# Sparse attention and a residual MLP on one core: w_tok in two halves, an identity made on GpSimd, and the order of the opening and of the weave

## The chip, the core and the metric

One core of a Trainium2 chip. Its engines run side by side, each through its own queue in order: PE (TensorE: matmuls and transposes, with weight loads shown as PEld), DVE (VectorE), ACT (ScalarE), POOL (GpSimd) and SP (SyncE, which only issues DMAs here). ACT and POOL also issue DMAs from their queues. The metric is the device time in microseconds (us) of one execution.

## The reference, cut to what matters

```
scores = q @ k.T / 8            # 4 batches, 8 heads, 768 tokens, 64 dims
scores = where(mask, scores, -1e9)   # per 32x32 block: window of 1, first and last
                                     # block, and 3 sampled blocks in each row of blocks
x   = softmax(scores) @ v            # heads side by side: (4, 768, 512)
a1  = alpha1 * x + beta1
u   = x + lam * einsum('ts,bsd->btd', w_tok, a1)
a2  = alpha2 * u + beta2
out = u + lam * (relu(a2 @ w_ch1) @ w_ch2)
```

w_tok is 768 x 768; w_ch1 is 512 x 2048 and w_ch2 is 2048 x 512. All inputs are float32 in DRAM; the work is done in bfloat16 and float16 with float32 sums.

## The kernel before, in words

Tokens are held as 128 partitions x 6. The 32 heads are worked in 16 pairs, numbered from 0; four pairs make a batch. The whole program is one list of instructions, written out in an order that lists in the file decide.

**Pairs 0 to 4** make the first stage. Each pair has 9 units, so there are 45 steps (the loop over `s`, L1089). A step issues the scores of one unit on PE (`emit_qk`, L583: k is the weight, 88 rows deep, since 24 rows of mask levels and block indicators lie under the 64 of q and k), the exp of the unit on ACT (`emit_exp`, L601, 128 x 1024), and two steps later the product with v (PV, L630), with a column of ones in `vext` that gives the row sums. Two PSUM buffers (`sp`) hold the scores, so the scores of step s wait for the exp of step s - 2. A finished head is scaled on DVE (`emit_finish`, L670 and L671) and then made into `a1pp` (L687, L688), on DVE or POOL as `A1V` says.

Between these, `PLAN` places every other job of the stage: a name and a time in steps. A job runs in the step of its whole part, ahead of PV where the fraction is under 0.5 and behind it otherwise. Among these jobs are the loads (`emit_load`, by POOL), the transposes of q and k through PSUM (`emit_tps`, L493, evicted by DVE at L499), the casts of v (`emit_lay`, L313), the mask rows of the other buffers (`emit_mask_rows`, L439), the mask as columns for later (`emit_mask_cols`, L508, L511; spread by POOL at L519), the broadcast of lam, alpha1 and beta1 over partitions (`emit_parts`, `emit_bcast`, L719 to L730), the transposes of w_tok (`emit_wtok_t`, L778, L779), the token mix of pairs 0 to 3 (`job_tok`, L795 to L810), the transposes of u (`job_ut` at L846, or a DMA transpose with `emit_uscale` at L870), and the loads and scaling of w_ch1 and w_ch2 (`emit_w1_load` L753, `emit_w2_load` L759, `emit_w2_use` L765). `OPEN` and `POUR` say how many f1 jobs follow each of the last three steps.

**Pairs 5 to 15** make the second stage. Their scores are 64 rows deep, from DMA transposes (`emit_tdma`), and a mask of zeros and ones is multiplied in on DVE (`emit_keep`, L618). The strings of `WEAVE` set the order, a string to three units: q the scores, x an exp, k a mask product, p PV of one block of keys (L653), f one f1 job (4 matmuls of 384 columns, L884, relu on ACT at L891), g one f2 job (4 matmuls of 512, L903, added to x by DVE at L912), T two chunks of the token mix (L819), d and v DMA transpose and scaling of u, L, Q, K and Y loads and layouts of later pairs, 0, 1 and 2 the jobs that PLAN has in that slot.

**The opening** (before and around step 0) loads head 0 of q, k and v by SP and ACT, the sampled blocks by SP, and by ACT one constant of 128 x 640 bytes that holds the identity for transposes and the fixed part of the mask (L346). Nine filler matmuls run on PE meanwhile (`emit_warm(9)`, L463). q is cast on DVE, k on ACT; six transposes (`emit_tps0`, L481) follow, with DVE's copies (L471). DVE finds the mask of blocks (L394, L402), and six copies on ACT and three on DVE turn it into mask levels and spread them over the rows under k (`emit_mask_part`, L420 and L412). POOL makes the ones of `vext` (L363) and the indicator rows under q (L368, L370).

Tiles in PSUM come from pools: `sp` with two buffers, `mm` with three, `op` with one. In the first stage every second head sums into an `mm` buffer.

Of the kernel before, what the change touches and what calls it, by code (L numbers as in the profile page):

```python
# [20 lines left out]
S = 768  # L21
# [16 lines left out]
OPEN = 42  # L38
UTD = [1, 1]
TDM = [1, 0]  # L40
A1V = [1, 0, 0, 1, 0, 0, 0, 1]
POUR = [3, 1, 1]
W1 = [
    "q f Y x f 0 f p k 1 f k f p x 2 f f k f f",
    "q L f x Q f f f k p x f p 0 k 1 p k 2",
    "q x g x f k k f 0 g 1 g k 2 K",
    "q Y Q k p K g p x x 0 f 1 s k 2 p k L f",
    "q 0 f x x g 1 g g k p k k 2",
    "q k s g p f x 0 f k 1 T x f p 2 k",
    "q 0 1 f p x k 2 p K T x L k p k",  # L50
    "q f x f 0 x T 1 p 2 Y k p k k Q",
    "q x f 0 k k g p x 1 s 2 g k d g",
]
W2 = [
    "q 0 p p p f d L x K f k v g 1 Q v g k x g g k 2",
    "q x 0 k f x g s 1 k 2 T T p p k T",
    "q d Y k p x g 0 1 2 g d g k x v p k",
    "q k L g x k 0 p g g 1 x p k 2 Q v",
    "q g x p g 0 x f f f Y k 1 f k 2 k f",
    "q 0 f k p x k f p f f f x 1 p p K f k f 2",  # L60
    "q f f x f f k 0 1 Q Y x p k g g 2 k s",
    "q 0 g g s k x f f 1 f 2 x k L f k p p",
    "q T f T T k 0 1 x x k K f f 2 f k p f f",
    "q p p p d s k x L d 0 x K k g k Y 1 f f 2 g",
    "q 0 x k Q g x 1 g p k 2 k p",
    "q k x v 0 1 p g k x k f g f g 2",
]
W3 = [
    "p p p f g v f s g T T T g g d g g g g d g g v g v g g f f f f f f",
    "f f f f f f f f f f f f g f f g f g f g f f g g f g f f g f f g g g f g",  # L70
    "f f g g g g g g g g g g g g",
]
WEAVE = W1 + W2 * (B - 2) + W3
ENG = {
# [16 lines left out]
    "tq1": 0,  # L91
}
PLAN = {
    "layv00": 0.29,
    "wtkl": 0.42,
    "warm1": 0.49,
    "loadv2": 0.58,
    "layk01": 1.22,
    "layq01": 1.25,
    "mask_cols": 1.5,  # L100
    "rows1": 2.08,
    "tps0": 2.52,
    "parts": 2.83,
    "mask1": 2.94,
    "w1_0": 2.96,
    "tq1": 4.55,
    "layv01": 4.3,
    "rows2": 4.5,
    "tk1": 4.82,
    "lv1": 5.01,  # L110
    "bcast0": 5.1,
    "rows3": 5.84,
    "loadk3": 6.08,
    "bcast2": 6.12,
    "loadv3": 7.02,
    "mask3": 7.41,
    "loadk2": 8.21,
    "loadq2": 8.52,
    "bcast1": 8.8,
    "loadq3": 9.23,  # L120
    "a1pp0": 9.37,
    "w1_2": 9.64,
    "w1_1": 10.3,
    "columns": 11.32,
    "wt2": 11.35,
    "wt1": 11.76,
    "wt5": 12.19,
    "lv2": 12.84,
    "wt4": 13.01,
    "wt0": 13.43,  # L130
    "loadv4": 13.94,
    "w1_3": 14.3,
    "tq2": 14.44,
    "loadq4": 14.54,
    "wt3": 15.31,
    "columns_use": 16.32,
    "tk2": 16.6,
    "tok0_0": 17.05,
    "tok0_1": 17.4,
    "tk3": 18.13,  # L140
    "loadk4": 18.23,
    "tok0_2": 20.0,
    "tq3": 20.4,
    "mask8": 20.72,
    "loadk5": 20.73,
    "mask2": 20.89,
    "tok0_3": 21.32,
    "tok0_4": 22.02,
    "lv3": 22.91,
    "mask6": 22.94,  # L150
    "mask0": 23.62,
    "tok0_5": 23.87,
    "loadq5": 24.3,
    "tok1_0": 24.53,
    "mask4": 24.64,
    "w2_0": 24.82,
    "mask7": 25.08,
    "lv4": 25.4,
    "tok1_1": 25.6,
    "tok1_2": 27.2,  # L160
    "loadv5": 27.53,
    "tok1_3": 27.74,
    "tok1_4": 28.91,
    "tok1_5": 29.7,
    "w2_2": 29.98,
    "mask5": 30.09,
    "tq4": 30.41,
    "mask15": 30.72,
    "udma0": 30.82,
    "tk4": 31.72,  # L170
    "udma1": 31.9,
    "w2_1": 32.02,
    "tq5": 32.51,
    "mask9": 32.65,
    "tok2_0": 33.91,
    "tk5": 34.64,
    "usc0": 34.69,
    "tok2_1": 34.88,
    "mask14": 34.9,
    "mask13": 35.48,  # L180
    "tok2_2": 35.71,
    "mask11": 35.79,
    "tok2_3": 36.37,
    "lam16": 37.24,
    "mask17": 37.68,
    "w2_3": 37.7,
    "mask16": 37.75,
    "tok2_4": 37.77,
    "mask10": 37.9,
    "tok3a_0": 38.34,  # L190
    "tok3a_1": 38.43,
    "tok2_5": 38.51,
    "tok3a_2": 38.52,
    "tok3a_3": 38.85,
    "tok3a_4": 39.48,
    "tok3b_0": 39.51,
    "tok3b_1": 39.52,
    "tok3b_2": 39.53,
    "tok3b_3": 39.54,
    "ut2": 39.85,  # L200
    "tok3a_5": 40.02,
    "mask12": 40.23,
    "tok3b_4": 40.23,
    "usc1": 40.28,
    "lv5": 40.42,
    "ut3_0": 40.8,
    "tok3b_5": 41.21,
    "cast3": 42.22,
    "lam2": 42.25,
    "lam3": 43.09,  # L210
    "ut3_1": 43.63,
    "lam1": 44.85,
    "lam10": 44.92,
    "lam9": 45.25,
    "lam7": 45.27,
    "lam0": 45.32,
    "lam11": 45.58,
    "lam6": 45.9,
    "lam13": 46.09,
    "lam5": 47.61,  # L220
    "lam14": 47.82,
    "lam4": 47.9,
    "lam8": 49.72,
    "lam12": 49.8,
    "lam15": 50.13,
}


# [1 line left out]
def kernel(  # L230
# [31 lines left out]
    kbi_np = np.tile(np.arange(NBLK, dtype=np.float32), (NBLK, 1))  # L262
    ms_np = np.concatenate([mstat_np] + [kbi_np] * NR, axis=1)

    const_np = np.zeros((P, P + 2 * (1 + NR) * NBLK), dtype=ml_dtypes.bfloat16)
    const_np[:, 0:P] = np.eye(P, dtype=ml_dtypes.bfloat16)
    const_np[0:NBLK, P:] = ms_np.view(ml_dtypes.bfloat16)
    const_dr = nc.inline_tensor(const_np, name="const_c")
    indq_dr = nc.inline_tensor(np.tile(indq_np, (1, 2)), name="indq_c")
    ident8_dr = nc.inline_tensor(np.eye(8, dtype=np.float32), name="ident8_c")  # L270

# [6 lines left out]
    def ptile(shape, dt, name):  # L278
        return pp.tile(shape, dt, name=name, tag=name)
# [4 lines left out]
    def copy_of(name):  # L284
        return (nc.vector.tensor_copy, nc.scalar.copy, nc.gpsimd.tensor_copy)[ENG[name]]
# [34 lines left out]
            :, 2 * n * NT * D : 2 * (n + 1) * NT * D  # L320
        ].rearrange("p (w x) -> p w x", w=2)
    sampi = ptile([P, 2 * NR], I32, "sampi")
    const = ptile([P, P + 2 * (1 + NR) * NBLK], BF, "const")
    identb = const[:, 0:P]
    ms = const[:, P:].bitcast(FP)
    NQB = 4
    qTs = [ptile([P, 2, S], BF, f"qTs{i}") for i in range(NQB // 2)]
    kTs = [ptile([P, 2, S], BF, f"kTs{i}") for i in range(NQB // 2)]
# [14 lines left out]
    load_first("q", q, 0, nc.sync)  # L343
    load_first("k", k, 0, nc.scalar)
    nc.sync.dma_start(sampi[0:NBLK, :], sampled_blocks.bitcast(I32))
    nc.scalar.dma_start(const[:], const_dr.ap())  # L346
    load_first("v", v, 0, nc.sync)
    load_first("k", k, 1, nc.scalar)
    load_first("q", q, 1, nc.sync)
# [9 lines left out]
        qTs[1][D : D + NBLK], indq_dr.ap().rearrange("r (w s) -> r w s", w=2)  # L359
    )  # L360
    warm = nc.const_aps.tensor(1.0, (P, DM), BF)
    for t in vexts:
        nc.gpsimd.memset(t[:, :, :, D : D + 1], 1.0)  # L363

    def emit_indicator():
        rows = qTs[0][D : D + NBLK]
# [37 lines left out]
        ms[0:NBLK, :].rearrange("q (r b) -> q b r", r=1 + NR),  # L404
        axis=mybir.AxisListType.X,
    )
    big = ptile([P, 1], FP, "big")
    nc.vector.memset(big[:], -BIG8)

    def level_rows(eng):  # L410
        if eng == 0:
            return lambda out, in_: nc.vector.tensor_scalar(  # L412
                out=out,
                in0=in_,
                scalar1=1.0,
                scalar2=BIG8,
                op0=ALU.subtract,
                op1=ALU.mult,
            )
        return lambda out, in_: nc.scalar.activation(  # L420
            out, in_, AF.Identity, bias=big[0:NBLK, :], scale=BIG8
        )

    def emit_mask_part(jp, copy):
        sl = kText[0][D : D + NBLK, ts(jp, 2 * P)]
        dst = sl.rearrange("q (o g r) -> q o g r", o=2, r=16)
        src = mbm[0:NBLK, :].rearrange("q (g m) -> q g m", m=3)
        m_of = (6 * np.arange(16) + 2 * jp) // BLK
        assert (m_of == (6 * np.arange(16) + 2 * jp + 1) // BLK).all()
        for m in range(3):  # L430
            lo, hi = np.searchsorted(m_of, [m, m + 1])
            shape = [NBLK, 2, NBLK // 3, int(hi - lo)]
            copy(
                out=dst[:, :, :, int(lo) : int(hi)],
                in_=src[:, :, m].unsqueeze(1).unsqueeze(3).broadcast_to(shape),
            )
# [14 lines left out]
    def mm_tile(shape=(P, DM), dt=FP):  # L451
        return psum.tile(list(shape), dt, name="mm", tag="mm", bufs=3)
# [316 lines left out]
    def emit_wtk_load():  # L769
        t = ap_.tile([P, NH, QC], BF, name="hts", tag="hts", bufs=2)  # L770
        wtks[0] = t[:, 0:12, :].rearrange("p (o w) n -> p o (w n)", o=NT)
        nc.gpsimd.dma_start(wtks[0], moe_w_tok.rearrange("(p o) s -> p o s", o=NT))

    def emit_wtok_t(os_):
        wtk = wtks[0]
        tps = mm_tile((P, NT, P), BF)
        for ot in range(NT):
            nc.tensor.transpose(tps[:, ot, :], wtk[:, ot, os_:S:NT], identb[:])  # L778
        nc.vector.tensor_copy(out=wtokT[:, os_, :], in_=tps[:])  # L779

    toks = {}
    ubfs = {}
# [203 lines left out]
            start_mlp(i // NP)  # L988

    emit_load(1)  # L990
    for m in (32, 64):
        nc.gpsimd.tensor_tensor(
            out=pick[0:96],
            in0=identb[0:96, 0:12] if m == 32 else pick[0:96],
            in1=identb[0:96, m : m + 12],
            op=ALU.add,
        )
    nc.gpsimd.memset(parts[:], 0.0)
    emit_mask_part(0, level_rows(ENG["mp0"]))
    emit_mask_part(1, level_rows(ENG["mp1"]))  # L1000
    emit_tps0(0)
    emit_warm(2)
    emit_mask_part(2, level_rows(ENG["mp2"]))

# [191 lines left out]
```

## Time and profile before

| | us |
|---|---|
| median of 3 runs (302.95 to 303.28) | 303.16 |
| the profiled execution | 303.09 |
| its span, first to last instruction | 301.4 |
| granted TensorE clock, mean | 0.998 |
| PE busy in the span | 295.3 |
| first exp on ACT starts | 7.36 |
| first scores of pair 5 on PE | 58.61 |
| last matmul of the program (L923) ends, about | 298.4 |

How to read it: "idle before" in a row is the time for which the engine did nothing ahead of the group, with what released it. A row of the timeline holds instructions of one kind in a row, so its second number is the length of the group, not of one. PE's busy time holds the fillers of the opening too, and the ends of matmuls are modelled; the distance of the starts of two matmuls tells more than their durations. Times between steps are therefore given from start to start.

### The profile page before, as it was taken

How to read it: one execution, taken by the hardware profiler on the slowest of the kernel's cores; microseconds unless marked ns; L12 is line 12 of the kernel's file. 1: busy time of each engine (PE TensorE's matmuls, PEld its weight loads, DVE VectorE, ACT ScalarE, POOL GpSimd, SP SyncE). 2: the span in 40 equal slices, each digit the busy share in tenths (PEclk: the TensorE clock that was granted, in tenths of full speed). 3: DMA queues.
4: the chain of work that ended last, by engine and by line, in shares of the span. 5: the costliest groups of instructions: out<-in, count | busy, mean ns of one | idle time of the engine just before them, and what ended most of it. 6: DMA issues, size and time to landing. Idle time of an engine off the chain costs nothing.

```text
span 301.4 us, 7199 instructions
## 1 busy us (share of the span) xinstructions
PE 295.3 (98%) x2976; PEld 184.5 (61%) x2996; DVE 193.1 (64%) x372; ACT 215.3 (71%) x314; POOL 113.1 (38%) x150
## 2 busy tenths in 40 slices
PE   8999999999999999999999999999999999999996
PEld 3687888655567556565665556565675664555543
DVE  3998799887758899845377779854476872000012
ACT  4999997999879775889778774889868610663310
POOL 8989589344328422613408501703206300000000
PEclk9999999999999999999999999999999999999999
DMA  6999999918297697970746693880411004100011
GB/s 191 188 198 204 204 165 186 155 29 129 68 132 115 111 140 120 130 159 2 115 78 111 115 171 89 124 165 3 63 32 23 37 35 122 37 0 35 37 70 70
DMA packets 57892, 31.34 MB, mean 104 GB/s; under 512 B 37952, under 2 KB 54764, under 8 KB 57732
## 3 DMA queue, kind: packets, MB, share of 16 engines
q0 software_dynamic: 16608, 14.22, 32.1%
q1 hardware_dynamic: 40820, 16.19, 25.5%
q10 hardware_dynamic: 432, 0.48, 0.5%
q8 instruction: 23, 0.38, 0.5%
q14 instruction: 9, 0.07, 0.1%
HBM read 29.83 MB, written 6.29 MB: 120 GB/s over the span
## 4 chain that ended last, share of the span: by engine, by line
PE 94%; ACT 3%; DMA 1%; issue 1%; DVE 0%; ACTq 0%
PE mm L884 28%; PE mm L903 26%; PE sp L583 10%; PE op L653 8%; PE mm L819 8%; PE mm L583 4%; PE mm L795 3%; ACT eT L601 2%; PE op L630 2%; DMA const<-const_c 1%; PE mm L923 1%; PE mm L630 1%; PE mm L493 1%; PE mm L778 1%; ACT kTs L420 1%
## 5 line engine op out<-in xcount | busy, mean ns | idle before, releaser
L601 ACT ACTIVATE eT<-sp,expb 128x1024 f16<-128x1024 f32 x111 | 118.4, 1118 | 3.0 <-PE sp L583 2.5
L891 ACT ACTIVATE hts<-mm 128x384 bf16<-128x384 f32 x128 | 62.1, 496 | 47.9 <-PE mm L884 47.1
L884 PE MATMUL mm<-uT,w1b 128*128 128x384 bf16 x512 | 92.6, 326 | 0.0
L618 DVE TENSOR_TENSOR eT<-eT,mask 128x1024 f16<-128x1024 f16 x99 | 74.8, 779 | 26.2 <-ACT eT L601 26.0
L903 PE MATMUL mm<-w2b,hts 128*128 128x512 bf16 x348 | 85.7, 379 | 1.1
L687 POOL TENSOR_TENSOR a1pp<-x_sb,vbc 128x384 bf16<-128x384 f32 x27 | 32.7, 1211 | 123.1 <-DVE x_sb L671 118.8
L884 PEld LDWEIGHTS <-w1b 128*128 128x128 bf16 x512 | 48.1, 98 | 35.0 <-issue 3.4
L903 PEld LDWEIGHTS <-hts 128*128 128x128 bf16 x368 | 34.0, 98 | 38.7 <-issue 4.0
L601 ACT ACTIVATE eT<-mm,expb 128x512 f16<-128x512 f32 x66 | 41.8, 686 | 18.5 <-PE mm L583 18.2
L912 DVE TENSOR_TENSOR ot<-x_sb,mm 128x512 f32<-128x512 f32 x23 | 15.7, 684 | 45.4 <-PE mm L903 45.4
L653 PEld LDWEIGHTS <-eT 128*128 128x128 f16 x792 | 29.6, 98 | 8.7 <-issue 1.5
L653 PE MATMUL op<-vext,eT 128*128 128x65 f16 x792 | 31.7, 194 | 0.0
L688 POOL TENSOR_TENSOR a1pp<-a1pp,vbc 128x384 bf16<-128x384 bf16 x27 | 27.3, 1009 | 2.1
L583 PE MATMUL sp<-qTs,kTs 88*128 88x512 bf16 (+1 forms) x120 | 27.0, 326 | 0.9 <-ACT eT L601 0.7
L819 PE MATMUL mm<-a1pp,wtokT 128*128 128x256 bf16 x216 | 25.6, 273 | 0.0
L819 PEld LDWEIGHTS <-wtokT 128*128 128x128 bf16 x216 | 20.8, 98 | 4.2 <-ACT hts L891 0.8
L583 PE MATMUL sp<-qhT,khT 64*128 64x256 bf16 (+1 forms) x176 | 19.7, 322 | 0.0
L630 PEld LDWEIGHTS <-eT 128*128 128x128 f16 x360 | 15.0, 97 | 3.7
L583 PEld LDWEIGHTS <-khT 64*128 64x128 bf16 x264 | 10.5, 94 | 10.9 <-issue 6.8
L831 DVE TENSOR_TENSOR x_sb<-x_sb,mm 128x512 f32<-128x512 f32 x18 | 12.3, 685 | 7.1 <-PE mm L819 6.8
L671 DVE TENSOR_TENSOR x_sb<-op,rcp 128x384 f32<-128x384 f32 x28 | 15.6, 557 | 1.0
L837 DVE CAST ubf<-x_sb 128x256 bf16<-128x256 f32 (+1 forms) x44 | 13.7, 347 | 0.9
(92 smaller groups left out, 225.5 us busy)
## 6 DMA issues: line engine op xcount, KB each, us to landing
out_dram<-ot SPq DMA_DIRECT2D x23, 256.0 KB
qpad<-in_q_dram POOLq DMA_DIRECT2D x15, 192.0 KB, 3.8
kr<-in_k_dram POOLq DMA_DIRECT2D x15, 192.0 KB, 5.7
vr<-in_v_dram POOLq DMA_DIRECT2D x15, 192.0 KB, 6.0
w1b<-in_moe_w_ch_dram POOLq DMA_DIRECT2D x4, 512.0 KB, 10.9
w2b<-in_moe_w_ch_dram POOLq DMA_DIRECT2D x4, 512.0 KB, 6.6
hts<-in_moe_w_tok_dram POOLq DMA_DIRECT2D x1, 1152.0 KB, 10.6
x_sb<-in_k_dram ACTq DMA_DIRECT2D x2, 192.0 KB
```

The costliest lines, as they stand in the source:

```text
L583: nc.tensor.matmul(sp[jj][:, dst], lhsT, rhs, start=True, stop=True, skip_group_check=True,)
L601: nc.scalar.activation(dst, at, AF.Exp, bias=expb[:], scale=SCALE)
L618: nc.vector.tensor_mul(out=e, in0=e, in1=keep)
L630: nc.tensor.matmul(op[0][:, o, :], ets[u][:, jj, h * QB + n * P : h * QB + n * P + P], vexts[i % NVB][:, w, 2 * jp + jj, :], start=op[1] == 0,
L653: nc.tensor.matmul(op[0][:, o, :], ets[u][:, jj, h * QB + n * P : h * QB + n * P + P], vexts[i % NVB][:, w, 2 * jp + jj, :], start=op[1] == 0,
L687: eng.tensor_tensor(out=dst, in0=x_sbs[b][:, :, cols], in1=bc[0], op=ALU.mult)
L688: eng.tensor_tensor(out=dst, in0=dst, in1=bc[1], op=ALU.add)
L819: nc.tensor.matmul(ps[:, o], wtokT[:, os_, ts(2 * n + o, P)], a1pps[i][:, os_, :], start=(os_ == 0 and o == 0), stop=(os_ == NT - 1 and o ...
L884: nc.tensor.matmul(ps[:, 0:QC], w1b[:, dk, ts(n, P)], uTs[b][:, dk, ts(c, QC)], start=(dk == 0), stop=(dk == 3),)
L891: nc.scalar.activation(hts[(b, c)][:, n, :], ps[:, 0:QC], AF.Relu)
L903: nc.tensor.matmul(ps[:], ht[:, nk, ts(o % 3, P)], w2b[:, nk, :], start=(nk == 0), stop=(nk == NH - 1),)
L912: nc.vector.tensor_tensor(out=ot[:], in0=x_sbs[b][:, o, :], in1=ps[:], op=ALU.add)
```

## The change

- **w_tok.** The load by POOL (1152 KB as bfloat16) is split into two, each with half of the tokens that a partition holds. Transposes are regrouped: a set of six now takes one half of the tokens t and two of the six residues s, so three sets need the first load alone. The eviction still writes 768 columns.
- **Identity.** It is no longer part of the constant. POOL sets a 128 x 128 tile to ones and selects the diagonal, in the place of the ones of `vext`, which move behind the loads of pair 1. ACT loads the fixed part of the mask alone, 24 rows of 384 bytes.
- **Mask levels.** One instruction on DVE turns the mask of blocks into levels (`mbs`, 24 x 24), and the nine copies only spread them. The constant `big` goes.
- **Fillers.** One less between the transposes of head 0 and the first scores.
- **Lists.** `A1V`, `POUR`, `PLAN` and `WEAVE` have new values. Among them: both casts of v go ahead of the mask columns; the mask columns' transposes go behind the third unit of scores; rows of buffer 2 and the parts of lam go to POOL ahead of the loads of pair 2; the first set of w_tok's transposes goes ahead of the scores of step 11; ut2 goes from step 39 to 37; two quarters of w_ch1 are loaded at steps 39 and 41; four f1 jobs instead of five stand before pair 5; a1pp of pair 2's first head goes from POOL to DVE.

The diff, cut to its core:

```diff
-A1V = [1, 0, 0, 1, 0, 0, 0, 1]
-POUR = [3, 1, 1]
+A1V = [0, 0, 0, 1, 1, 0, 0, 1]
+POUR = [-19, 2, 2]
 W1 = [
-    "q f Y x f 0 f p k 1 f k f p x 2 f f k f f",
-    "q L f x Q f f f k p x f p 0 k 1 p k 2",
+    "q x L 0 k p f 1 2 f f x p f f f k p K f k",
+    "q Y 0 f 1 k p 2 x f f f x f k k p f g",
...
 W3 = [
-    "p p p f g v f s g T T T g g d g g g g d g g v g v g g f f f f f f",
+    "p p p f g s g T T T g g d d v g g g g g g v g g g f f f f",
...
 PLAN = {
-    "layv00": 0.29,
-    "layk01": 1.22,
-    "layq01": 1.25,
-    "mask_cols": 1.5,
-    "rows1": 2.08,
-    "tps0": 2.52,
-    "layv01": 4.3,
-    "rows2": 4.5,
-    "tk1": 4.82,
+    "layq01": 0,
+    "layk01": 0.75,
+    "rows2": 0.76,
+    "layv01": 1,
+    "layv00": 1.07,
+    "parts": 1.58,
+    "mask_cols": 2.56,
+    "rows1": 2.6,
+    "tps0": 2.98,
+    "tk1": 5.6,
...
-    "w1_2": 9.64,
-    "w1_1": 10.3,
-    "wt2": 11.35,
-    "wt1": 11.76,
-    "wt5": 12.19,
-    "wt4": 13.01,
-    "wt0": 13.43,
-    "w1_3": 14.3,
-    "wt3": 15.31,
-    "tok0_0": 17.05,
+    "wt0": 10.75,
+    "wt1": 11.35,
+    "wt2": 11.37,
+    "wt3": 13.34,
+    "wt4": 13.64,
+    "wt5": 13.82,
+    "tok0_0": 15.09,
+    "w1_1": 30.27,
+    "w1_2": 39.72,
+    "w1_3": 41.39,
...
-    const_np[:, 0:P] = np.eye(P, dtype=ml_dtypes.bfloat16)
-    const_np[0:NBLK, P:] = ms_np.view(ml_dtypes.bfloat16)
-    const_dr = nc.inline_tensor(const_np, name="const_c")
+    ms_dr = nc.inline_tensor(ms_np, name="ms_c")
...
-    nc.scalar.dma_start(const[:], const_dr.ap())
+    nc.scalar.dma_start(ms[0:NBLK, :], ms_dr.ap())
...
-    for t in vexts:
-        nc.gpsimd.memset(t[:, :, :, D : D + 1], 1.0)
+    nc.gpsimd.memset(identb[:], 1.0)
+    nc.gpsimd.affine_select(
+        out=identb[:], in_=identb[:], pattern=[[-1, P]],
+        compare_op=ALU.is_equal, fill=0.0, base=0, channel_multiplier=1,
+    )
...
+    mbs = ptile([P, NBLK], BF, "mbs")
+    nc.vector.tensor_scalar(
+        out=mbs[0:NBLK, :], in0=mbm[0:NBLK, :],
+        scalar1=1.0, scalar2=BIG8, op0=ALU.subtract, op1=ALU.mult,
+    )
...
-        nc.gpsimd.dma_start(wtks[0], moe_w_tok.rearrange("(p o) s -> p o s", o=NT))
+        src = moe_w_tok.rearrange("(p o) s -> p o s", o=NT)
+        for o in (slice(0, 3), slice(3, NT)):
+            nc.gpsimd.dma_start(wtks[0][:, o], src[:, o])
...
-    def emit_wtok_t(os_):
-        tps = mm_tile((P, NT, P), BF)
-        for ot in range(NT):
-            nc.tensor.transpose(tps[:, ot, :], wtk[:, ot, os_:S:NT], identb[:])
-        nc.vector.tensor_copy(out=wtokT[:, os_, :], in_=tps[:])
+    def emit_wtok_t(n):
+        h, o2 = divmod(n, 3)
+        tps = mm_tile((P, 2, 3, P), BF)
+        for os_ in range(2):
+            for ot in range(3):
+                nc.tensor.transpose(
+                    tps[:, os_, ot, :],
+                    wtks[0][:, 3 * h + ot, 2 * o2 + os_ : S : NT], identb[:],
+                )
+        nc.vector.tensor_copy(
+            out=wtokT[:, 2 * o2 : 2 * o2 + 2, ts(h, 3 * P)],
+            in_=tps[:].rearrange("p s o q -> p s (o q)"),
+        )
...
-    emit_mask_part(0, level_rows(ENG["mp0"]))
-    emit_mask_part(1, level_rows(ENG["mp1"]))
+    emit_mask_part(0, copy_of("mp0"))
+    emit_mask_part(1, copy_of("mp1"))
     emit_tps0(0)
-    emit_warm(2)
+    emit_warm(1)
```

## The prediction

> **What bounds the kernel now.** I read the page first, then the busy time by stretches, then the timelines of ACT, DVE and PE over the opening and the first stage. The page:
>
> ```profile
> PE 295.3 (98%) x2976; PEld 184.5 (61%) x2996; DVE 193.1 (64%) x372; ACT 215.3 (71%) x314; POOL 113.1 (38%) x150
> ...
> PE   8999999999999999999999999999999999999996
> ...
> PE 94%; ACT 3%; DMA 1%; issue 1%; DVE 0%; ACTq 0%
> ```
>
> The chain that ends last is 94% PE, so PE sets the end. A share is only an average, so the stretches follow (columns: length, busy time of PE, PEld, DVE, ACT, POOL, clock, DMA share, GB/s):
>
> ```profile
> 10.00:20.00 10.00, 9.31 (x149) 7.44 (x148) 9.17 (x21) 9.97 (x11) 8.30 (x16) 1.00 1.13 202
> ...
> 60.00:100.00 40.00, 39.90 (x417) 24.84 (x418) 31.00 (x57) 36.51 (x59) 18.04 (x19) 1.00 0.60 96
> ...
> 200.00:290.00 90.00, 89.58 (x701) 52.58 (x705) 36.55 (x67) 49.40 (x86) 11.70 (x10) 1.00 0.18 43
> ```
>
> From 60 us on PE is full, and its matmuls start one behind the other (512 columns every 0.216 us, 384 every 0.162). Nothing there can be won; a new weave can only lose. From 10 to 50 us ACT and DVE are as full as PE. ACT in that stage:
>
> ```profile
> 5.69 1.65 ACT L420 ACTIVATE kTs<-mbm,big 24x96 bf16<-24x96 f32 x6 [1.15 <-DVE big L408]
> 7.36 14.64 ACT L601 ACTIVATE eT<-sp,expb 128x1024 f16<-128x1024 f32 x14
> 22.24 4.14 ACT L601 ACTIVATE eT<-sp,expb 128x1024 f16<-128x1024 f32 x4 [0.24 <-PE sp L583]
> 26.91 18.80 ACT L601 ACTIVATE eT<-sp,expb 128x1024 f16<-128x1024 f32 x18 [0.52 <-PE sp L583]
> ...
> 49.48 1.11 ACT L601 ACTIVATE eT<-sp,expb 128x1024 f16<-128x1024 f32 x1 [0.36 <-PE sp L583]
> 51.69 3.32 ACT L601 ACTIVATE eT<-sp,expb 128x1024 f16<-128x1024 f32 x3 [1.08 <-PE sp L583]
> ```
>
> The first stage is 45 steps of one exp each, 1.02 us apart where ACT sets the pace (starts at 37.43, 38.45, 39.47). The gaps in brackets are where ACT waits for PE: the work on PE between two score matmuls was over 1.02 us for several steps running. So stage one ends late for two reasons: it starts at 7.36 us, and PE's work is spread unevenly. The opening on PE and DVE:
>
> ```profile
> 5.09 0.80 PE L481 MATMUL mm<-const,qk 128*128 128x128 bf16 x6 [0.25 <-DMA const<-const_c]
> 5.68 1.06 PE L463 MATMUL op<-const-bfloat16-1.0 128*128 128x512 bf16 x2
> 6.62 0.68 PE L583 MATMUL sp<-qTs,kTs 88*128 88x512 bf16 x2
> ...
> 18.26 0.83 PE L778 MATMUL mm<-const,hts 128*128 128x128 bf16 x12
> ```
>
> ```profile
> 5.07 0.22 DVE L394 TENSOR_TENSOR const<-sampi,const 24x72 f32<-24x72 int32 x1 [0.96 <-DMA const<-const_c]
> 5.33 0.30 DVE L402 TENSOR_REDUCE mbm<-const 24x24 f32<-24x96 f32 x1
> ...
> 17.86 0.56 DVE L671 TENSOR_TENSOR x_sb<-mm,rcp 128x384 f32<-128x384 f32 x1
> 18.80 1.66 DVE L779 COPY wtokT<-mm 128x768 bf16<-128x768 bf16 x3 [0.38 <-PE mm L778]
> ```
>
> PE's transposes and the mask on DVE both wait for the constant transfer (landed 5.05). From 5.71 to 18.42 DVE has no gap at all: it is a second bound of the opening.
>
> **The change, part by part.** The profiled execution took 303.09 us for a span of 301.4, so 1.7 lie around the span; I leave those alone. It is 0.07 below the median of 303.16.
>
> *Identity by GpSimd, mask constants alone.* PE's transposes now wait for the k casts on ACT (3.94 to 4.54) and for the ninth filler, issued at 4.21 and 0.43 long: they start at 4.64 instead of 5.09, 0.45 earlier. GpSimd has the identity ready long before: a memset and a select of 128 columns in the place of three ones-memsets (0.26); a select of 768 columns took 0.9, so 128 are bounded by 0.9 and end before 3. The small mask transfer isn't in the trace; the q load of 192 KB landed 2.9 after its issue, const 3.8, so it lands at 4.1 to 5.05 and I take 4.2, nearest the smaller load. The reduce then ends near 4.7 and the new one-off scaling (24x24, 0.1 by L412's 0.17 for 24x80) near 4.8; ACT's six mask copies (0.275 each) end at 6.5 instead of 7.34.
>
> The first scores wait for DVE's copies of q and k: 5.26 + 0.42 + 0.24 = 5.93, so they go at 6.05 (before 6.62). Here is the limit: matmuls of 512 columns went every 0.427 us up to about 6.8 and every 0.216 after. At half rate the two end at 7.1; at full rate at 6.65. The first exp starts between 6.6 and 7.1, and 6.9 is taken: **-0.46** (bounds -0.75 and -0.25). The removed filler lies in this gap and costs nothing more.
>
> *w_tok in halves.* The whole load landed at 17.9 (issued 7.4, 10.6 to land) and its first transposes ran at 18.26. At the 202 GB/s of that stretch a half (576 KB) takes 2.9, so the first half is in at 15.0, and its first six transposes move ahead of score matmul 11, at about 16.9. The 36 transposes and the six evictions of 768 columns stay as many. One more DMA issue on POOL (0.58) sits ahead of v2's load; POOL waits there anyway.
>
> *The pieces placed anew.* I counted PE's work between score matmuls in both orders (0.436 a unit of scores, 0.0305 a PV matmul, 0.056 one of 128 columns, 0.0285 one of 64). Up to step 10 the new order holds 9.70 us against 9.37, up to step 37 it holds 38.92 against 38.25: tok, ut2 and the transposes moved up into steps where PE waited for ACT. So steps 38 to 44 hold 9.75 instead of 11.07. ACT needs only 7.1 for these seven, so PE sets their pace and 1.32 come off; 0.65 of that is one f1 job (16 matmuls of 384 columns instead of 20 before pair 5's first scores), to be paid later at full price. The rest, **-0.67**, is a gain. Part goes back: steps 13 and 15 now hold 1.68 and 1.56 (before 1.35 and 0.89), more than ACT's 1.02, and delay exps 14 to 18 by some **+0.14**.
>
> *Waits that it adds.* First, the second w_tok transpose needs the buffer of the head finished on DVE (17.86 to 18.42 before). It was to go at 18.6; now at 17.6. DVE starts 0.45 earlier, but now casts both v pieces before the mask columns, and those wait for transposes moved behind score unit 2 (9.0 instead of 8.5), so DVE is at that finish only 0.1 to 0.4 earlier. PE waits 0 to 0.5 there, with score matmul 12 behind it: **+0.2**, taken at DVE's earlier start. Second, the first f1 now follows the last transposes of u by one score unit. Its fourth matmul waits for DVE: add, cast, scale, add, evict (0.57, 0.5, 0.6 to 0.98, 0.57, 0.5), 2.9 to 3.3 after the tok matmul that releases them; PE gets there after 2.7. 0.2 to 0.6 by the sum, nothing if DVE runs ahead: **+0.15**.
>
> *Loads.* Two quarters of w1 go out near 48 and 50 us instead of at 20 to 24. w1 landed 10.9 after issue, a w2 quarter issued at 48.55 after 5.8; they are in by 54 to 61, and f1 needs them at 60.7 and 65. Cost nothing, cover 0 to 6 us.
>
> *Later weave.* PE's work is the same but for the f1 job. The shortest stretch between a finished head and the next one in the same PSUM bank falls from 1.95 to 1.30 us of PE work; reciprocal and scaling took 0.2 + 0.56, so it still holds. DMA transposes have over 8 us in hand. Nothing.
>
> Sum: -0.46 - 0.67 + 0.14 + 0.2 + 0.15 = **-0.64**. 303.09 - 0.64 = 302.45 for such an execution, 302.5 for the median.
>
> **The rivals.** *DVE holds the opening.* Exp 0 comes only at 7.1, and both DVE waits cost in full: -0.25 - 0.53 + 0.5 + 0.3 = 0.0, so 303.1. For it: DVE's gapless 12.7 us, and that exp 12 would start at 19.65, as before (19.66). Against: the 0.67 of PE work moved up is untouched by it. It includes the case that the halved load doesn't help since PE isn't ready for it.
>
> *The clock comes late* (slower). PE's half rate ended at 6.8 before, after steady fillers. With one filler less, PE idles from 5.66 to 6.05. If that keeps the rate at half through steps 0 to 3, their 3.27 us of PE work become 6.5 against 4.1 on ACT: +2.4, less the 0.64 gives 304.9. It decides if PE idles more before 6.8 than the 0.45 that it already did (4.64 to 5.09); the new gap is 0.4, so it is unlikely. The Trainium skill (TensorE: Matmul & The Clock Gate, Part 1) says that the gate opens only after a busy window of 3.4 us and that its windows run free of the kernel. By that rule a missed window would last until 10.2 us, and what a single filler does would change from run to run. The half-rate rows here agree with the gate; no row shows a missed window.
>
> *w1 lands late* (slower). POOL is held by waits for buffers ahead of these loads; if they leave 3 us later and take 10.9, PE waits for f1's third quarter until 62.5 or later: +1.5 to 2, so about 304.
>
> *Neither wait bites and the rate rises early*: -0.75 - 0.53 = 301.8.
>
> **How the numbers follow.** A measurement of this kernel can tell about 0.2%, 0.6 us. The forecast has 0.36 and the better case 0.10, so faster 0.46. DVE holding the opening, and what of the forecast falls short of 0.6, have 0.37 (same). The clock has 0.09, the late w1 0.08 (slower 0.17). Leaving out the clock's case and the outer half of the better and of the late one (0.18 in all), the range is 301.7 to 304.0.
>
> **What would show it.** Transposes of q and k at 4.6 to 4.7, ACT's exps from 6.6 to 7.1, w_tok transposes before 17.3 (right), or a gap of PE ahead of the second set at 17.6 to 18.3 with DVE as its releaser (first rival); the first scores of pair 5, at 58.6 now, at 57.3 with one f1 job less done. Wrong altogether if PE shows gaps after 60 us, or 0.43 us matmuls after 7.

## The result, and the profile after

The changed kernel took 302.01 us (median of 6 runs, 301.77 to 302.49) against 303.20 for the kernel before beside it: a ratio of 0.9957, 95% interval 0.9946 to 0.9969. A second set gave 0.9954 (0.9942 to 0.9967). So it is faster by 0.43%; 302.5 and "faster" were forecast, with 301.8 for the case that neither wait bites. That better case is what came: the gain is 1.2 us, where the forecast had 0.6.

The page after. PE still sets the end, with 2 us less of busy time:

```profile
PE 293.2 (98%) x2970; PEld 183.2 (61%) x2995; DVE 195.6 (65%) x374; ACT 212.7 (71%) x314; POOL 112.0 (37%) x151
...
PE   7999999999999999999999999999999999999996
...
PE 94%; ACT 3%; DMA 1%; issue 1%; DVE 0%; ACTq 0%
```

The busy time by stretches. From 10 to 20 us PE now works 9.82 of 10 us (9.31 before); after 60 it is as full as it was:

```profile
10.00:20.00 10.00, 9.82 (x150) 7.70 (x148) 8.75 (x20) 9.93 (x11) 9.35 (x16) 1.00 1.14 199
60.00:100.00 40.00, 39.79 (x410) 24.37 (x413) 29.94 (x55) 35.71 (x57) 15.60 (x17) 1.00 0.54 87
200.00:290.00 90.00, 89.42 (x680) 52.13 (x686) 35.66 (x65) 47.44 (x83) 12.87 (x13) 1.00 0.21 49
```

ACT in the opening and the first stage (start, length, line, tiles, count, and in brackets the wait ahead of it):

```profile
5.34 1.08 ACT L432 COPY kTs<-mbs 24x96 bf16<-24x96 bf16 x6 [0.78 <-DVE mbs L412]
6.63 14.44 ACT L600 ACTIVATE eT<-sp,expb 128x1024 f16<-128x1024 f32 x14 [0.21 <-PE sp L582]
21.67 13.69 ACT L600 ACTIVATE eT<-sp,expb 128x1024 f16<-128x1024 f32 x13 [0.59 <-PE sp L582]
35.56 15.98 ACT L600 ACTIVATE eT<-sp,expb 128x1024 f16<-128x1024 f32 x15 [0.20 <-ACT eT L600]
51.80 2.20 ACT L600 ACTIVATE eT<-sp,expb 128x1024 f16<-128x1024 f32 x2 [0.26 <-PE sp L582]
```

The first exp starts at 6.63 instead of 7.36. The gap of 1.08 us that stood before the exp at 51.69 is gone, and 0.26 is left of it. PE and DVE at the places that the prediction named:

```profile
4.42 0.51 PE L480 MATMUL mm<-ident,qk 128*128 128x128 bf16 x6 [0.17 <-ACT qk L310]
...
5.99 0.60 PE L582 MATMUL sp<-qTs,kTs 88*128 88x512 bf16 x2 [0.84 <-ACT kTs L432]
```

```profile
16.59 0.54 PE L780 MATMUL mm<-ident,hts 128*128 128x128 bf16 x6
16.96 0.60 PE L582 MATMUL sp<-qTs,kTs 88*128 88x256 bf16 x4
17.40 0.83 PE L780 MATMUL mm<-ident,hts 128*128 128x128 bf16 x12
18.07 0.60 PE L582 MATMUL sp<-qTs,kTs 88*128 88x512 bf16 x2
```

```profile
16.95 0.56 DVE L670 TENSOR_TENSOR x_sb<-mm,rcp 128x384 f32<-128x384 f32 x1
17.42 1.54 DVE L785 COPY wtokT<-mm 128x768 bf16<-128x768 bf16 x3
```

The transposes of w_tok stand right behind a score matmul, with no bracket: PE waits neither for the load nor for DVE. DVE ends the finish of head 1 at 17.51 (16.95 + 0.56). The third set, the second half of the twelve transposes between 17.40 and 18.07, takes the buffer that this frees, and starts at about 17.74. So the slack there is some 0.23 us.

Where the time went, from the starts of the same instructions in both traces (after minus before, us):

```
exp 0      exp 38     first scores of pair 5    last matmul    span
-0.73      -0.74      -2.07                     -1.31          -1.30
```

The lead at exp 38 is that of exp 0. In between it moved from 0.34 (exp 17) to 1.05 (exp 10), since the two lists put PE's work in different steps; experiment 2 compares the same lists. Steps 38 to 44 give 1.32 more (9.27 us instead of 10.59 from exp 38 to the first scores of pair 5), of which one f1 job (0.65) is paid back in the second stage, which also lost 0.10.

### The profile page after: what moved, and what is told of

It reads as the page before. It is cut to its first block, busy times and chain, and to the rows that moved or that the text cites. A ratio compares the mean times of both kernels' runs of the same rounds, so it can differ in the third digit from the quotient of the medians.

```text
span 300.1 us, 7192 instructions
## 1 busy us (share of the span) xinstructions
PE 293.2 (98%) x2970; PEld 183.2 (61%) x2995; DVE 195.6 (65%) x374; ACT 212.7 (71%) x314; POOL 112.0 (37%) x151
## 4 chain that ended last, share of the span: by engine, by line
PE 94%; ACT 3%; DMA 1%; issue 1%; DVE 0%; ACTq 0%
PE mm L891 28%; PE mm L910 26%; PE sp L582 10%; PE op L652 9%; PE mm L826 8%; PE mm L582 4%; PE mm L802 3%; ACT eT L600 2%; PE op L629 2%; PE mm L629 1%; PE mm L930 1%; DMA ms<-ms_c 1%; PE mm L780 1%; PE mm L492 1%; PE mm L532 0%
## 5 line engine op out<-in xcount | busy, mean ns | idle before, releaser
L898 ACT ACTIVATE hts<-mm 128x384 bf16<-128x384 f32 x128 | 60.9, 500 | 42.1 <-PE mm L891 41.5
L617 DVE TENSOR_TENSOR eT<-eT,mask 128x1024 f16<-128x1024 f16 x99 | 80.2, 840 | 15.9 <-ACT eT L600 15.7
L910 PE MATMUL mm<-w2b,hts 128*128 128x512 bf16 x343 | 84.4, 379 | 1.3 <-issue 0.3
L686 POOL TENSOR_TENSOR a1pp<-x_sb,vbc 128x384 bf16<-128x384 f32 x26 | 29.7, 1141 | 124.2 <-DVE x_sb L670 94.7
L670 DVE TENSOR_TENSOR x_sb<-op,rcp 128x384 f32<-128x384 f32 x28 | 15.6, 558 | 1.0
```

Source lines behind the costliest of these rows:

```text
L617: nc.vector.tensor_mul(out=e, in0=e, in1=keep)
L686: eng.tensor_tensor(out=dst, in0=x_sbs[b][:, :, cols], in1=bc[0], op=ALU.mult)
L898: nc.scalar.activation(hts[(b, c)][:, n, :], ps[:, 0:QC], AF.Relu)
L910: nc.tensor.matmul(ps[:], ht[:, nk, ts(o % 3, P)], w2b[:, nk, :], start=(nk == 0), stop=(nk == NH - 1),)
```

## The experiments

Ratios are to the kernel before, run on the same chip.

**1. The opening alone.** The kernel before, its lists and its single load of w_tok, with only the opening changed:

```diff
-    nc.scalar.dma_start(const[:], const_dr.ap())
+    nc.scalar.dma_start(ms[0:NBLK, :], ms_dr.ap())
...
+    nc.gpsimd.memset(identb[:], 1.0)
+    nc.gpsimd.affine_select(out=identb[:], in_=identb[:], ...)
...
+    nc.vector.tensor_scalar(out=mbs[0:NBLK, :], in0=mbm[0:NBLK, :], ...)
...
-    emit_warm(2)
+    emit_warm(1)
```

> The opening of the changed kernel (identity by GpSimd, mask constants alone, mask scaled once, one filler fewer) with the lists and the w_tok load of the kernel before. My theory: the first exp comes at 6.6 as in the changed kernel and nothing later eats it, since ACT and PE share the bound to 50 us: 303.2 - 0.73 = 302.5 (302.3 to 302.8), and step for step the exps lie 0.6 to 0.75 earlier than before. Rival (DVE holds the opening): DVE's gapless 12.7 us sets exp 12 at 19.66 as before, and the time is 303.0 to 303.2.

Measured: 303.43 us, ratio 1.0008 (0.9999 to 1.0017). The opening alone is worth nothing. Exps 0 to 5 lie 0.56 earlier than before; from exp 6 on all lie 0.23 to 0.25 later. Two views of this kernel (PE, then GpSimd) show why:

```profile
11.33 0.60 PE L582 MATMUL sp<-qTs,kTs 88*128 88x512 bf16 x2
12.60 0.38 PE L718 MATMUL mm<-parts,pick 96*128 96x128 bf16 x4 [0.68 <-POOL parts L713]
...
13.07 0.60 PE L582 MATMUL sp<-qTs,kTs 88*128 88x512 bf16 x2
```

```profile
1.08 0.29 POOL L359 TENSOR_SCALAR_AFFINE_SELECT ident<-ident 128x128 bf16<-128x128 bf16 x1
...
6.90 0.28 POOL L991 MEMSET vext<- 128x12 f16 x3
...
10.58 0.28 POOL L709 CAST parts<-vrows 12x128 bf16<-12x128 f32 x1
...
12.13 0.42 POOL L713 TENSOR_TENSOR parts<-rest,part 12x128 bf16<-12x128 f32 x1
```

PE is ready for the broadcast of lam 0.56 earlier, stands 0.68 us for the parts that GpSimd makes, and score matmul 6 stands behind it. In the kernel before (GpSimd, then PE) the last operation on the parts ended at 12.03 and PE came at 12.32, so there the slack was 0.29 us and no view of waits showed it:

```profile
11.61 0.42 POOL L714 TENSOR_TENSOR parts<-rest,part 12x128 bf16<-12x128 f32 x1
```

```profile
12.32 0.39 PE L719 MATMUL mm<-parts,pick 96*128 96x128 bf16 x4
```

The slack was used up from both sides. PE came 0.56 earlier, and GpSimd was done 0.52 later (12.55 instead of 12.03), mostly because the same edit gives it the select of the identity (0.29) at the start and puts the three memsets of ones (0.28) behind the loads of pair 1, ahead of the parts. 0.56 + 0.52 - 0.29 = 0.79 is what the exps lose at step 6 (from 0.56 early to 0.23 late). The earlier start alone would have lost 0.27 there. The end (carried or eaten) was the rival's, but the engine was not DVE: it was GpSimd.

**2. The lists and the halves alone**, with the old opening (the reverse: W1 to W3, PLAN, A1V, POUR and the two functions of w_tok of the changed kernel, in the kernel before).

> The kernel before with the changed lists and the halved w_tok, but the old opening (identity and mask constants in one transfer, two fillers). My theory: the lists are worth what is left beside the opening, 1.2 - 0.7 = 0.5: 302.7 (302.5 to 302.9), first exp at 7.36, first scores of pair 5 at 57.3. Rival: the lists need the earlier start (the DVE wait of 0.2 to 0.5 at the second set of w_tok transposes and the fourth f1 matmul come back): 303.0 to 303.3, with a gap of PE ahead of the second set. Second rival: the two parts overlap, and the lists alone reach 302.2 or less.

Measured: 302.73, ratio 0.9982 (0.9974 to 0.9991). That is my first theory's 302.7. From exp 38 to the first scores of pair 5 it takes 9.27 us (before 10.59, changed kernel 9.27): the moved pieces are worth 1.32 with or without the opening. Alone, the parts give +0.18 and -0.52 in medians; together they give -1.2.

Beside this run, which has the same lists, the changed kernel leads by 0.82 at exp 0 and still by 0.77 at exp 29: with these lists the opening's gain is carried. (The profiled execution here was the slowest of eleven, 303.54. At exp 30 it loses 0.3 where PE waits for a load of k, and it loses 0.3 more at the place near 195 us that experiment 5 shows.) The changed list puts the broadcast of lam one step later (6.34 instead of 5.1). PE comes there at 12.53 in the changed kernel, and GpSimd is done with the parts at 12.47: no slack is left, but no exp is late for it.

**3. The opening with the broadcast placed later.**

```diff
-    "bcast0": 5.1,
+    "bcast0": 6.34,
...
-    "bcast2": 6.12,
+    "bcast2": 7.37,
```

> open_alone with two list entries as the changed kernel has them: the first broadcast of lam (PE matmuls on the parts that GpSimd casts until 12.5) from step 5.1 to 6.34, the third one from 6.12 to 7.37. In open_alone PE stood 0.68 for those parts at 11.9 to 12.6 with score matmul 6 behind it, and exp 6 lost 0.80 of the 0.56 lead and more. My theory: this wait alone ate the opening; with it gone the exps keep a lead of 0.5 or more over the kernel before to step 12 and most of it to the end: 302.5 to 302.8. Rival: DVE, gapless from 5 us on, takes the lead away by step 13 (w_tok's whole load lands at 17.9 and its transposes stand at 18.3 as before): 303.0 to 303.3.

Measured: 302.99, ratio 0.9996 (0.9986 to 1.0006). Now the lead of 0.56 lives to exp 8, and then falls to 0.10 at exp 9 and stays there. Here it is DVE, the rival's engine, though four steps earlier than the rival had it:

```profile
15.64 0.38 PE L718 MATMUL mm<-parts,pick 96*128 96x128 bf16 x4 [0.29 <-DVE vbc L727]
```

PE's next broadcast waits for DVE's evict of the first one (L727, 14.90 to 15.59). So in the old list two engines stood in line behind PE, GpSimd first and DVE second. In the changed kernel the same evict runs at 13.86, for there the copy of v1 on DVE comes behind it and not ahead of it, and the next broadcast stands at 9.0 instead of 8.8. Which of these entries frees DVE was not tested by itself.

**4. One load of w_tok**, all else as in the changed kernel:

```diff
-        for o in (slice(0, 3), slice(3, NT)):
-            nc.gpsimd.dma_start(wtks[0][:, o], src[:, o])
+        nc.gpsimd.dma_start(wtks[0], src)
```

> The changed kernel with w_tok in one load of 1152 KB again, transposes grouped and placed as in the changed kernel. My theory: the load lands at 17.5 to 18, PE stands at the first set from 16.6 on, so exp 12 comes 0.9 to 1.3 later; since PE is the bound of the stage most of it stays: 302.0 + 0.7 to 1.2 = 302.7 to 303.2. Rival: the wait is made up in steps where PE waits for ACT, as at exp 14: 302.0 to 302.3.

Measured: 304.10, ratio 1.0035 (1.0012 to 1.0058); the profiled execution took 303.2, 1.4 more than that of the changed kernel. The runs spread widely here (303.1 to 306.0, one at 308.5), which I can't explain. In the trace PE waits for the load:

```profile
17.51 0.54 PE L779 MATMUL mm<-ident,hts 128*128 128x128 bf16 x6 [0.66 <-DMA hts<-in_moe_w_tok_dram]
```

Exps lose 0.75 at step 11 and never get it back. That is about half of the 1.4. For the rest, exp 0 came 0.17 later here, 0.2 went at the place near 195 us (experiment 5), and the time behind the last matmul was 0.35 longer. So the halves are needed by the new place of the transposes. In the changed kernel itself the first half landed at 16.54 in the first trace and at 15.37 in another, with the transposes at 16.59 and 16.51. 15.0 was forecast; the cover is 0.05 and 1.1 us, so it is thin.

**5. The mask unscaled**: 400 in the indicator rows, 0 or 1 in the mask rows, 50 more subtracted in the exps of the first five pairs; one DVE operation less in the opening.

```diff
-    nc.vector.tensor_scalar(out=mbs[0:NBLK, :], in0=mbm[0:NBLK, :], ...)
...
-        nc.gpsimd.memset(first, 1.0)
+        nc.gpsimd.memset(first, BIG8)
...
-            nc.scalar.activation(dst, at, AF.Exp, bias=expb[:], scale=SCALE)
+            nc.scalar.activation(dst, at, AF.Exp, bias=(expm if u < N1 else expb)[:], scale=SCALE)
```

> The changed kernel without the one-off scaling of the mask on DVE (0.43 us of the chain reduce, scaling, mask copies on ACT): the indicator rows hold 400 in the place of 1, the mask rows 0 or 1, and the exps of the first five pairs subtract 50 in their bias, which gives the same weights. My theory: the first scores wait for ACT's mask copies, which start 0.35 to 0.43 earlier, until DVE's copies of q and k (ends 5.65 to 6.1) set them: exp 0 at 6.3 to 6.45, time 301.7 to 301.8. Rival: DVE's copies already set the first scores: 301.9 to 302.1. If the opening carries to the end at less than half, under 0.1 is seen.

Measured: 302.10 (301.84 to 303.01), ratio 0.9972 (0.9962 to 0.9982), no gain. Yet the mechanism held: exp 0 at 6.40, and the exps lead the changed kernel's first profile by 0.23 at the start, 0.14 at steps 8 to 10 and 0.32 at pair 5. The second stage lost it: the last matmul is 0.21 later. PE and DVE of this kernel near 195 us, then SP's queue in the changed kernel:

```profile
194.80 0.91 PE L644 MATMUL op<-vext,eT 128*128 128x65 f16 x24 [0.34 <-DVE x_sb L662]
```

```profile
192.36 0.48 DVE L869 TENSOR_SCALAR uT<-uraw,ab2T 128x768 bf16<-128x768 bf16 x1 [0.71 <-DMA uraw<-ubf]
```

```profile
187.57 0.34 SPq L922 DMA_DIRECT2D out_dram<-ot  x1
187.96 2.24 SPq L868 DMA_TRANSPOSE uraw<-ubf  x1
```

The transpose of u goes out at 187.96, behind a store, and DVE wants it at 192. DVE stands, then finishes the head late, and PE's PV matmuls need that head's bank. The stretch from exp 144 to exp 149 (counted over the whole trace) took 6.02 to 6.54 us in seven profiles with the changed lists: 6.02 in the first trace of the changed kernel, 6.37 in its second, 6.54 here. So from 0 to 0.5 us are lost there.

**6. The changed kernel again, and two edits beside it.**

> The changed kernel once more, unaltered, beside v_later and no_scale_v on one chip. Expected 302.0 (301.8 to 302.6). The trace tells how two things differ from run to run: when the half rate of 512-column matmuls ends (3.4 to 3.9 us in the first trace of this kernel), and how long DVE stands for the transposed u before its second scaling near 192 us (0.16 us in the first trace; 0.41, 0.49 and 0.71 in three kernels with the same lists).

Measured: 301.97 (301.75 to 302.10). Exp 0 at 6.63 again; the half rate ended at 4.8 this time (3.7 in the first trace); DVE stood 0.54 us for u.

```diff
-    "q 0 p k x v Q v 1 2 p k x g k g",
+    "q 0 p k x v Q 1 2 p k x v g k g",
```

> The changed kernel with the second v of the fourth list of W2 (the scaling of a transposed u on DVE) four pieces later. My theory: in the changed lists that v comes so soon behind its transpose on SP's queue (issued 187.96, landed 192.1) that DVE stands and the PV matmuls of the next head with it, 0.0 to 0.5 us on PE from run to run; with it later no such gap is left near 192 to 197 us, and the time is 301.8 with less spread: 0.1 to 0.3 under the changed kernel beside it. Rival: DVE's masks behind the v get later in other places, or the wait moves to the first f1 of the batch: same as the changed kernel or slower by up to 0.5.

Measured: 301.92, ratio 0.9951 (0.9939 to 0.9964), not to be told from the kernel beside it. The wait for u is gone, and that stretch takes 6.02 us in all four profiles with this edit (this one, no_scale_v below, and experiments 7 and 8), so the cause is settled. The time did not show it, since this profile lost 0.4 us elsewhere, for GpSimd's parts again (done at 12.99 here, at 12.47 and 12.57 in the two profiles of the changed kernel):

```profile
13.04 0.38 PE L718 MATMUL mm<-parts,pick 96*128 96x128 bf16 x4 [0.51 <-POOL parts L713]
```

> Both edits: the mask unscaled, and the second v later. My theory: the 0.3 us by which no_scale led up to pair 5 (lost again at 192 to 197 us) is now kept: 301.4 to 301.6. Rival: the gap near 195 us comes back in another form, for work there hangs on transfers whose time is not PE's: 301.9 to 302.1.

Measured: 301.83 (301.60 to 301.96), ratio 0.9948 (0.9935 to 0.9960): the fastest version, but within the error of the changed kernel. Exps 0 to 6 lead those of the changed kernel's second profile by 0.30; ahead of exp 7 PE waits 0.43 us for the parts, and 0.02 is left. So in this profile GpSimd takes the earlier start away. It does not always: in no_scale PE waited 0.19 there and most of the lead lived on. The moment at which GpSimd is done with the parts (12.38 in no_scale, 12.55 here, 12.99 in v_later) moves more from profile to profile than the edit is worth.

**7. The parts earlier**, on top of no_scale_v:

```diff
-    "parts": 1.58,
+    "parts": 0.6,
```

> no_scale_v with GpSimd's five small operations on parts (1.95 us) moved in the list from 1.58 to 0.6, ahead of the load of v2 and of the copy of mask rows. My theory: the earlier opening of the changed kernel meets GpSimd next: PE stood 0.43 and 0.51 us ahead of score matmul 7 for parts in two of the runs, and lost the 0.3 us of no_scale there. With parts done near 10.8 instead of 12.5 that wait is gone, exps 7 to 11 keep the 0.3 lead over the changed kernel, and the time is 301.4 to 301.6 (0.3 under no_scale_v). Rival: DVE is next (its evict of the first broadcast, its copies of kTs), so the lead goes one step later: 301.8, with a gap of PE that DVE releases between 12.5 and 17 us. Second rival: v2's load or the mask rows now come 1.95 us late and are missed: 302 or more.

Measured: 301.98, ratio 0.9951 (0.9938 to 0.9964). The wait for the parts is gone (they are done at 11.29, and PE comes at 12.47). But this profile had no lead to keep: exp 0 came at 6.79, not at 6.34 as in no_scale_v, for ACT's cast of k ran 0.38 later and the transposes of q and k went at half rate until 5.1. So the forecast of 301.4 to 301.6 was not put to the test. What the trace does show is the rival's engine: DVE is next. The wait that the prediction had priced at 0 to 0.5 us shows itself, 0.36 ahead of the third set of w_tok transposes (1.19 for twelve, 0.83 without a wait), and exp 12 loses 0.3:

```profile
17.46 1.19 PE L772 MATMUL mm<-ident,hts 128*128 128x128 bf16 x12
18.48 0.60 PE L574 MATMUL sp<-qTs,kTs 88*128 88x512 bf16 x2
```

```profile
17.49 0.56 DVE L662 TENSOR_TENSOR x_sb<-mm,rcp 128x384 f32<-128x384 f32 x1
17.97 1.47 DVE L777 COPY wtokT<-mm 128x768 bf16<-128x768 bf16 x3
```

DVE frees the buffer at 18.05 instead of 17.51.

**8. DVE relieved** (the last of the chain):

```diff
-    "lv1": 8.63,
+    "lv1": 10.6,
```

> parts_early with one more entry: the copy of v1 on DVE (0.35 to 0.64 us) from step 8.63 to 10.6, behind the finish of head 1 instead of ahead of it. In parts_early PE stood 0.37 us inside the third set of w_tok transposes (17.46 to 18.48 for 12, against 0.84 in the changed kernel), since the PSUM buffer of head 1 came free on DVE only at 18.05. My theory: DVE is the next bound behind GpSimd's parts, and with 0.35 to 0.64 less ahead of that finish it ends at 17.4 to 17.6, the 12 transposes take 0.84 again, exp 12 starts at 18.3 to 18.6 and the time is 301.4 to 301.7. Rival: the copies of w_tok, now 0.35 later on DVE, hold PE at the next step, or another engine's limit is there at once: 301.9 to 302.1, with exp 13 no earlier than in the changed kernel (19.9).

Measured: 303.03 (302.22 to 305.54), ratio 0.9996 (0.9978 to 1.0014): the whole gain lost. DVE's finish ends at 17.52 and the twelve transposes take 0.84, as the theory said. But the copy of v1 also frees the buffer of the next v load. GpSimd waits to issue that load, and behind it stands the product that tok needs:

```profile
18.09 0.72 POOL L301 DMA_DIRECT2D vr<-in_v_dram  x1 [1.66 <-DVE vext L312]
18.82 1.01 POOL L678 TENSOR_TENSOR a1pp<-x_sb,vbc 128x384 bf16<-128x384 f32 x1
19.91 0.93 POOL L679 TENSOR_TENSOR a1pp<-a1pp,vbc 128x384 bf16<-128x384 bf16 x1
```

```profile
22.86 0.49 PE L794 MATMUL mm<-a1pp,wtokT 128*128 128x128 bf16 x6 [0.70 <-POOL a1pp L679]
```

Exps lose 0.86 at step 16 and more at step 30 to 32. I had not counted what the moved step releases.

**9. The pieces back in their old places** (34 due times of tok, ut and their transposes; two of them):

```diff
-    "tok0_0": 15.09,
+    "tok0_0": 17.05,
...
-    "ut2": 37.77,
+    "ut2": 39.85,
```

> The changed kernel with the due times of tok, ut and their transposes (34 entries) as in the kernel before; all else, the opening, the halves, two f1 jobs fewer, is kept. Counted from the built program, PE's work up to step 37 is then 38.25 us as in the kernel before (38.92 in the changed one), and steps 38 to 44 hold 10.42 instead of 9.75. My theory (the term of -0.67 with the +0.14 taken back): first scores of pair 5 0.5 to 0.7 later, 302.0 + 0.5 to 0.7 = 302.5 to 302.7. Rival: the early steps had no room for those pieces after all (they delayed exps one for one), so it makes no difference: 301.9 to 302.2. Second rival: ut3 and its transposes now come so late that f1 waits on DVE: 303 or more.

Measured: 304.85, ratio 1.0047 (1.0034 to 1.0060): the second rival's price, but not its cause, for no f1 matmul waits for DVE. Exp 36 is 0.67 later than in the changed kernel's second profile, exp 40 3.15. It doesn't measure the term alone: due times of one order in another made PE wait for DVE (0.35 ahead of a tok piece at 46.36) and left it idle for 1.5 us more between 10 and 56 us (busy 44.33 of 46 against 45.82 in the changed kernel). What it shows is only that the old places do not fit the new order; the term itself is read from the steps (below).

**10. One filler instead of nine.**

```diff
-    emit_warm(9)
+    emit_warm(1)
```

> The changed kernel with one 512-column filler at the start instead of nine, so that PE is idle from about 1.3 to 4.4 us. It prices the rival of the late clock. By that rival a half rate through steps 0 to 3 costs up to 2.4 us: 304.4. Milder: PE's steps 0 to 6 hold 0.44 to 1.0 us of work at full rate against 1.02 of ACT, at half rate 0.9 to 2.0, so if the rate rises one window of 3.4 us after the transposes (at 8 to 9) only the first scores (0.4) and steps 2 and 3 (0.9 each over) are late: 302.0 + 0.8 to 1.5. If neither is seen (302.0 to 302.2), the fillers do nothing and the clock's rival was empty.

Measured: 305.03 (303.61 to 305.97), ratio 1.0045 (1.0019 to 1.0070). In the profiled execution the matmuls run at half rate from 4.8 until about 15.6 us:

```profile
4.77 0.82 PE L480 MATMUL mm<-ident,qk 128*128 128x128 bf16 x6 [3.34 <-DVE ms L398]
...
14.33 1.06 PE L582 MATMUL sp<-qTs,kTs 88*128 88x512 bf16 x2
```

Two score matmuls still take 1.06 us at 14.33, against 0.60 at 5.99 in the changed kernel. Exps lie 0.70 late at step 0 and 4.0 at step 6, where ACT is the pace again. So the price of the late clock was of the right size (2.4 forecast; 3.0 by the medians, 1.6 to 4.0 by the runs), though the half rate lasted beyond the steps 0 to 3 of that rival. Only its condition did not come: in all thirteen other profiles, with nine fillers, the full rate had come by 6.8 us.

## Why the prediction was right, point by point

- **What bounds it.** Right: after 60 us nothing was won. But the reading "from 10 to 50 us ACT and DVE are as full as PE" holds for DVE only from 10 to 20 us and from 40 to 50 (8.50 and 8.01 of 10 us in the stretches between), and it missed GpSimd, which was busy for 8.30 us from 10 to 20 and for 9.82 from 20 to 30, and had a slack of 0.29 us to PE.
- **Opening, -0.46.** Mis-sized: -0.73, near the outer bound. The first scores went at 5.99, as forecast (6.05), but not at half rate: in the first trace the full rate came at 3.7 us, in before at about 6.8. Where it came late (5.2 to 6.2 in open_alone, open_bcast and one_load) exp 0 was at 6.80, -0.56. Both lie within the bounds. The way there was partly another: the last to be ready were ACT's mask copies (0.84 in the view above), not DVE's copies of q and k. The new scaling took 0.43 instead of 0.1, and the six copies took 1.08 instead of 1.65, so that two wrong sizes nearly cancelled: the copies ended at 6.42, where 6.5 had been forecast.
- **That the opening's gain is carried.** The sum took it for granted. It does not hold in the old list (open_alone), nor with two broadcasts moved (0.10 of 0.56 left in open_bcast); it holds with all of the new lists (0.82 to 0.77 beside lists_alone). The prediction had no term for the broadcasts, nor for the 0.5 us by which its own edit delays GpSimd. That the sum was in range with this step unseen was luck.
- **One more DMA issue, "POOL waits there anyway".** Misread: no view shows GpSimd waiting between 4.4 and 13 us, before or after. With one load, the parts are done at 12.18 instead of 12.47. It cost PE nothing here, as the parts were still just in time.
- **Pieces moved up, steps 38 to 44: -1.32.** Right: 1.32 in the changed kernel and in lists_alone; 0.65 of it was paid back. The first scores of pair 5 came at 56.5, where 57.3 had been named as the sign.
- **Taken back, +0.14.** About 0: the exps lie 0.73 earlier at step 0 and 0.74 at step 38. Steps 13 and 15 cost ACT 0.59 once (the exp at 21.67), but before had its own gap (0.24 and 0.52 at 22.24 and 26.91).
- **DVE wait at the w_tok transposes, +0.2.** Mis-sized: 0. DVE came to the finish 0.9 earlier, where I had 0.1 to 0.4, and it is the third set, not the second, that takes its buffer. The edge is real: the slack is 0.23, and parts_early pays 0.36 there.
- **f1's fourth matmul, +0.15.** 0: scores 44 follow scores 43 by 1.74 us, and two f1 jobs of 0.65 stand between; no bracket.
- **Loads of w1.** Right, no wait.
- **Later weave, nothing.** Failed in a part that I had called safe: "DMA transposes have over 8 us in hand" is not true of the fourth list of W2, where DVE comes 4.0 us after the issue. It cost 0 to 0.5 from profile to profile, and nothing in the one compared here. The 0.10 that the second stage lost beside the f1 job I can't place; the four profiles with the v later have it too.

In sum -0.73 - 1.32 + 0.65 + 0.10 = -1.30, against -0.64 forecast: both waits and the take-back were taken 0.49 too dear together, the opening's gain 0.27 too small, the later weave 0.10 too cheap. So direction and range were right, and the middle of the forecast was half of what came. The range of 301.7 to 304.0 held it, at its lower end; the case that came had been given 0.10. I think this was too little because each of its parts was judged apart, while the two waits both hang on how far DVE is.

**Rivals.** "DVE holds the opening" comes true in the old list (open_bcast), once GpSimd, which held it first (open_alone), is out of the way. The late w1 did not come. The clock: the Trainium skill (TensorE: Matmul & The Clock Gate, Part 1) puts the rise about one window of 3.4 us after the load begins, and says the windows run free of the kernel. Nine fillers from 0.85 gave the full rate between 3.7 and 6.8 us, which agrees in kind, with a wide spread. One filler does not agree: PE had no gap from 7.1 to 15.2 us, over two such windows, and stayed at half rate.

## What to carry to other kernels

A gain at the start is worth what the nearest engine behind lets through: for each wait that does not show, note how long ago its releaser was done (here 0.29 us), subtract what the edit itself adds to that engine (here 0.52), and take the smallest. Price a moved step by what it releases as well as by what it waits for, since a copy that frees a load's buffer holds the whole queue that issues the load. If a start-up edit seems worthless alone, try it together with the order that follows it before dropping it; here +0.18 and -0.52 made -1.2.

## What the runs showed of the hardware

- The granted clock stood at 1.00 in no_fill while its matmuls of 512 columns went every 0.427 us, in this stretch for one (the third figure from the end):

```profile
8.00:12.00 4.00, 4.00 (x30) 2.34 (x29) 2.52 (x9) 2.81 (x4) 3.73 (x8) 1.00 1.20 203
```

  The half rate of an opening is read from the spacing of matmuls, not from that column.
- The six mask copies took 1.08 us as COPY on ACT from bf16, and 1.65 as ACTIVATE with scale and bias from f32.
